# Which half of a block's queries and keys comes last: piece order and GpSimd's copies in a segment-recurrent attention kernel

## The chip, the cores and the metric

The kernel runs on one core of a Trainium2 chip. The metric is the device time of one execution in microseconds (us). The core's engines each follow an instruction stream of their own and meet through semaphores: TensorE (PE; its weight loads are shown as PEld), VectorE (DVE), ScalarE (ACT), GpSimd (POOL) and SyncE (SP). DMAs are issued from the queues of SP and GpSimd.

## The reference

The input x is 2048 x 512, in bf16. Two kinds of layer alternate, each twice: x + A(layernorm(x)), then x + B(layernorm(x)).

Layer A is attention over segments with a recurrent memory. The 2048 tokens are cut into 64 segments of 32. A memory of 8 rows stands ahead of each segment. Cut to what matters:

```python
for s in range(64):
    h = concat([mem, x[32*s:32*s+32]])          # 40 rows
    q, k, v = (einsum('btd,dhe->bhte', h, W) for W in (Wq, Wk, Wv))   # 32 heads of 128
    p = softmax(where(mask, q @ k.T * scale, -1e9))
    o = einsum('bhte,hed->btd', p @ v, Wo)
    mem, out[s] = o[:8], o[8:]
```

The memory that segment s + 1 reads is the result of segment s, so the 64 segments form a chain. Only the memory rows depend on the segment before: queries, keys and values of token rows can be computed ahead.

Layer B is a gated MLP: a projection with a GELU, a layernorm of one half, a 2048 x 2048 product over the rows, a product with the other half, and a projection back.

## The kernel before

One program does A, B, A, B. `a_block` is layer A and `b_block` layer B; the change lies in `a_block`, so it acts in both passes over it.

**Segments and blocks.** `a_block` loops over the 64 segments s. Four of them make a block of 128 tokens (`tb = s // 4`, `j4 = s % 4`); there are 16 blocks. The function `segment` computes one segment with all 32 heads. The heads are handled as two halves of 16 (r = 0 and 1). A segment works on a window of 32 rows: the 8 memory rows and the first 24 token rows. The last 8 token rows of each segment don't pass through this window: they are gathered over the four segments of a block (`hB`, 32 rows) and projected for the whole block ahead of time. The text calls that result a block's queries, keys and values: QTB, KTB and VB, both halves in each.

**Scores.** `scores(r)` makes the scores of half r on TensorE: sixteen small matmuls (L975) whose moving operand is QQ, all 40 query columns of a head, and four (L979) with the stationary operand KX[r], the last 8 keys of the segment. Each segment calls `scores(0)`, does a part of the value projection, and calls `scores(1)`. The mask product (`close`, L987, VectorE) and the sums and values follow.

**What fills QQ and KX.** Columns 0 to 31 of QQ come from the window, by a VectorE transpose in `qk_T` (L952). Columns 32 to 39 and KX come from the block's QTB and KTB, by three copies in `prep_segment`: QQ (both halves of the queries in one instruction, L905), KX[0] and KX[1] (L909). They run on GpSimd (for the very first segment of the program on VectorE). QQ and the two KX exist twice and alternate with the segments, so the copies for segment s + 2 can begin when segment s has made its scores.

**The pieces.** A block's projections are six pieces, numbered j: 0 and 1 are the halves of the queries, 2 and 3 the halves of the keys, 4 and 5 the halves of the values. A piece is sixteen matmuls (`b_mms`, L714, tile psb); ScalarE copies the result to `rowsB` (L763), and it is transposed into QTB or KTB in one of two ways: by a DMA transpose that SP issues (L768), or by VectorE (L766, called a turn; it is put on the list `turns`, and `run(turns)` near the end of the segment issues it). The pieces are written out by generators. A segment calls `fill()` three times, and each call runs its generator to the next `yield`; so pieces are spread over the four segments of the block before the one that will use them. `b_even` serves blocks 0 to 3 of a pass (which prepare 1 to 4), except the first pass's block 0: seven block boundaries in all. In each pair of segments one piece is "quartered", its four contraction steps at the first two fills of each segment, and two pieces are whole, each at the third fill. The whole piece at the last fill of a block is the one that VectorE turns. From block 4 on `b_units` does it, with another spread, and every piece is transposed by DMA.

Before the change the last two segments of `b_even` hold piece 2 (quartered), piece 1 (whole, by DMA) and piece 3 (whole, turned).

**What sets the order of instructions.** On TensorE, VectorE and ScalarE the order is the program's own, written out by hand (`ORDERED`, `tc.manual_schedule`). On GpSimd and SP the framework's scheduler sets it, within what the data dependencies allow; each engine then issues in that order and waits at the head of its queue.

Of the kernel before, what the change touches and what calls it, by code (L numbers as in the profile page):

```python
# [16 lines left out]
KT = 4  # L17
# [564 lines left out]
def qk_rhs(w, j, kt, cg):  # L582
    return w[j // 2][:, kt, :].rearrange("p (r gs i eb el) -> p r eb i gs el", r=2, gs=4, i=4, eb=4)[:, j % 2, cg]


def cols_rhs(w, j, kt, cg):
    at = 2048 * (j % 2) + 512 * cg
    return w[j // 2][:, kt, at:at + 512]
# [81 lines left out]
def a_block(tc, c, rows, front, MV_in, RS_in, MV_out, RS_out, ahead, wo, S, first):  # L670
# [6 lines left out]
    with ExitStack() as ctx:  # L677
# [34 lines left out]
        def mm_chunk(ps, lhs, rhs, kts=range(KT)):  # L712

            return [nc.tensor.matmul(ps[32 * cg:32 * cg + 32, :], lhsT=lhs(kt, cg), rhs=rhs(kt, cg), start=(kt == 0), stop=(kt == KT - 1),  # L714
                                     tile_position=(0, 32 * cg)) for kt in kts for cg in range(4)]
# [10 lines left out]
        QQr = [pers.tile([P, 2, 8, 40, 2], BF16, name=f"QQ{i}") for i in range(NKQ)]  # L726
        KXr = [[pers.tile([P, 4, 32], BF16, name=f"KX{i}{r}") for r in range(2)] for i in range(NKQ)]
        uT = [pers.tile([P, H, 32], BF16, name=f"uT{i}") for i in range(2)]
# [8 lines left out]
        def store_v(bs):  # L737
            nc.sync.dma_start(rows.vb_d[:], bs["VB"].rearrange("p i r e -> p (i r e)"))
# [8 lines left out]
        copies, turns, adds = [], [], []  # L747
# [5 lines left out]
        def b_out(bs, slot, j, ps, turned, stored):  # L753

            if j >= 4:
                nc.scalar.copy(bs["VB"][:, :, j - 4, :], ps.rearrange("p (i e) -> p i e", i=4))
                if turned:
                    ahead.regroup(bs["VB"], bs["VX"], (j - 4,))
                elif stored:
                    store_v(bs)  # L760
                return
            r = rowsB[:, slot, :]
            nc.scalar.copy(r, ps)  # L763
            t = bs[("QTB", "KTB")[j // 2]][:, j % 2]
            if turned:
                turns.append(lambda: nc.vector.transpose(out=t.rearrange("p a b -> p (a b)"), in_=r))  # L766
            else:
                nc.sync.dma_start_transpose(out=t.rearrange("p (i g) k -> p i (g k)", g=4), in_=r.rearrange("t (i e) -> t i e", i=4))  # L768

        def b_mms(bs, j, ps, kts, turned=False):  # L770
            mm_chunk(ps, lambda kt, cg: bs["hB"][:, kt, :],
                     lambda kt, cg: qk_rhs(w, j, kt, cg) if j < 4 and turned else cols_rhs(w, j, kt, cg), kts)
# [23 lines left out]
        def b_even(tb):  # L796

            bs = blk_state[tb]
            for j, others in ((4, (5, 0)), (2, (1, 3))):
                psA = accA.tile([P, 512], F32, name="psb")[:]  # L800
                for kt, other in zip((0, 2), others):
                    b_mms(bs, j, psA, (kt,))
                    yield
                    b_mms(bs, j, psA, (kt + 1,))
                    if kt == 2:
                        copies.append(lambda j=j, psA=psA: b_out(bs, 0, j, psA, False, True))
                    yield
                    psB = accB.tile([P, 512], F32, name="psb")[:]
                    b_mms(bs, other, psB, range(KT), other == 3)
                    copies.insert(0, lambda other=other, psB=psB: b_out(bs, 1, other, psB, other == 3, False))  # L810
                    yield

        def wo_pairs(px, lhs):
# [87 lines left out]
        def prep_segment(s, eng=nc.gpsimd):  # L901
            tb, j4 = s // 4, s % 4
            bs = blk_state[tb]
            QQ = QQr[s % NKQ]
            eng.tensor_copy(QQ[:].rearrange("p r n q two -> p (r n) two q")[:, :, :, 32:40],  # L905
                            bs["QTB"].rearrange("p r (n two) k -> p (r n) two k", two=2)[:, :, :, 8 * j4:8 * j4 + 8])
            KX = KXr[s % NKQ]
            for r in range(2):
                eng.tensor_copy(KX[r][:].rearrange("p g (k i) -> p i g k", i=4),  # L909
                                      bs["KTB"][:, r].rearrange("p (i g) k -> p i g k", i=4)[:, :, :, 8 * j4:8 * j4 + 8])  # L910
            seg_state[s] = dict(QQ=QQ, KX=KX, VX=bs["VX"])

# [19 lines left out]
        def segment(s, fill, spare1, spare2, spare3, tail, loads):  # L932
            tb, j4 = s // 4, s % 4
            st = seg_state.pop(s)
            QQ, KX, VX = st["QQ"], st["KX"], st["VX"]
            KA = KAr[s % 2]
# [20 lines left out]
            def ends(q):  # L957

                return q.rearrange("p h (b e) -> p h b e", e=8)[:, :, 0:5:4, :]

            def own(q):

                return q.rearrange("p (i b e) -> p i b e", i=4, b=2)
# [4 lines left out]
            def scores(r):  # L968
# [8 lines left out]
                for g in range(4):  # L977
                    q = QQ[:, r].rearrange("p (i g) q two -> p i g two q", i=4)[:, :, g // 2, g % 2, :]
                    mms.append(nc.tensor.matmul(own(pS[32 * g:32 * g + 32, 160:224]), lhsT=KX[r][:, g, :], rhs=ends(q),  # L979
                                                start=False, stop=True, tile_position=(0, 32 * g), skip_group_check=True))  # L980
# [162 lines left out]
            if s + 1 < NSEG:  # L1143
                prep_segment(s + 1)
# [14 lines left out]
        start = nc.vector if first else nc.gpsimd  # L1159
        rows.begin(start)  # L1160
        prep_segment(0, start)
        due, ys = [], []
        seen = pers.tile([P, 1], BF16, name="seen")
# [16 lines left out]
        for s in range(NSEG):  # L1180
            tb, j4 = s // 4, s % 4
# [149 lines left out]
```

## Time and profile before

| | |
|---|---|
| three runs, median (lowest to highest) | 1624.81 us (1623.7 to 1625.13) |
| the profiled execution | 1621.89 us |
| its span | 1620.2 us |
| granted TensorE clock, mean | 0.998 |
| TensorE busy | 1577.7 us, 97% |
| VectorE busy | 1070.7 us, 66% |
| ScalarE busy | 1050.1 us, 65% |
| GpSimd busy | 288.2 us, 18% |

The profile is of one execution. Times in it count from the start of its span; the execution's own time has some 1.7 us more around it. A row of the view in order of time reads: start in us, duration in us, engine, line of the kernel, operation, what it writes <- what it reads, partitions x elements, how many instructions are merged, and in brackets how long the engine sat idle before it and what ended that. A row of the waits reads: who waited <- for whom: us in total, times, longest. A row of the groups reads: busy us, mean ns of one | idle before it. "POOL" is GpSimd, "SPq" the queue of SyncE. Buffer numbers are left out of names; "old" and "front" are the memory that QTB, KTB and VB of odd and even blocks lie in, so "KX<-old" is a key copy and "old<-rowsB" a transposed piece.

Segment s of a pass begins its scores at the first of its L975 matmuls. Segments of the first blocks take 9.67 us each.

### The profile page before, as it was taken

How to read it: one execution, taken by the hardware profiler on the slowest of the kernel's cores; microseconds unless marked ns; L12 is line 12 of the kernel's file. 1: busy time of each engine (PE TensorE's matmuls, PEld its weight loads, DVE VectorE, ACT ScalarE, POOL GpSimd, SP SyncE). 2: the span in 40 equal slices, each digit the busy share in tenths (PEclk: the TensorE clock that was granted, in tenths of full speed). 3: DMA queues.
4: the chain of work that ended last, by engine and by line, in shares of the span. 5: the costliest groups of instructions: out<-in, count | busy, mean ns of one | idle time of the engine just before them, and what ended most of it. 6: DMA issues, size and time to landing. Idle time of an engine off the chain costs nothing.

```text
span 1620.2 us, 91261 instructions
## 1 busy us (share of the span) xinstructions
PE 1577.7 (97%) x41182; PEld 983.8 (61%) x41182; DVE 1070.7 (66%) x3059; ACT 1050.1 (65%) x2281; POOL 288.2 (18%) x604
## 2 busy tenths in 40 slices
PE   5899999999999999999999999999999999999999
PEld 2566666666666666566656656666666666665565
DVE  4576766667776776784366666666677667768622
ACT  3677777777777777660047777777777777776400
POOL 6111111112211221320011111111121112214000
PEclk9999999999999999999999999999999999999999
DMA  9412111113321333277952122121233223425696
GB/s 364 94 42 41 41 44 43 43 43 83 74 56 44 89 83 78 92 184 157 203 161 47 46 42 50 46 47 47 72 87 77 47 69 99 99 52 172 144 197 160
DMA packets 259805, 148.11 MB, mean 91 GB/s; under 512 B 193752, under 2 KB 235840, under 8 KB 259416
## 3 DMA queue, kind: packets, MB, share of 16 engines
q1 hardware_dynamic: 246184, 98.46, 27.8%
q0 software_dynamic: 13232, 43.82, 8.3%
q8 instruction: 322, 5.28, 1.4%
q14 instruction: 67, 0.55, 0.1%
HBM read 59.68 MB, written 37.19 MB: 60 GB/s over the span
## 4 chain that ended last, share of the span: by engine, by line
PE 50%; DMA 4%; DVE 2%; issue 0%; SPq 0%; ACT 0%; POOL 0%; DVEq 0%; ACTq 0%
PE psK L714 6%; PE psQ L714 6%; PE pg L397 5%; PE psb L714 5%; PE pz L296 5%; PE psO L825 4%; PE px L818 3%; PE psV L714 3%; PE psm L714 3%; PE pwB L837 2%; PE psO L1024 2%; PE psT L1016 1%; PE py L440 1%; DMA y_x<-xd 1%; DMA ln_x<-xd 1%; PE psS L975 1%
## 5 line engine op out<-in xcount | busy, mean ns | idle before, releaser
L714 PEld LDWEIGHTS <-hT 128*32 128x32 bf16 x12288 | 343.8, 97 | 265.3 <-DVE hT L924 14.0
L714 PE MATMUL psV<-Wv_sb,hT 128*32 128x512 bf16 x2048 | 165.7, 379 | 0.0
L952 DVE STREAM_TRANSPOSE QQ<-rows 128x256 f32<-128x256 f32 x256 | 113.1, 442 | 77.8 <-ACT rows L949 75.8
L949 ACT CAST rows<-psQ 128x512 bf16<-128x512 f32 x256 | 144.2, 592 | 27.6 <-PE psQ L714 24.9
L984 ACT ACTIVATE S<-psS 128x224 bf16<-128x224 f32 x256 | 92.2, 360 | 100.7 <-PE psS L979 100.5
L1045 DVE TENSOR_TENSOR uT<-psO,Rm 128x128 bf16<-128x128 f32 x256 | 74.7, 292 | 123.0 <-ACT Rm L1042 122.0
L397 PE MATMUL pg<-z,wspT 128*128 128x344 bf16 x1024 | 154.3, 309 | 0.0
L1048 DVE TENSOR_TENSOR uT<-psO,Rt 128x384 bf16<-128x384 f32 x256 | 140.4, 548 | 19.2 <-ACT Rt L1124 17.0
L952 DVE STREAM_TRANSPOSE KA<-rows 128x256 f32<-128x256 f32 x256 | 113.6, 444 | 59.5 <-ACT rows L949 56.4
L714 PE MATMUL psK<-Wv_sb,hT 128*32 128x512 bf16 x2048 | 152.0, 378 | 0.0
L1124 ACT ACTIVATE Rt<-Rt 128x512 f32<-128x512 f32 x256 | 147.3, 622 | 4.0
L825 PE MATMUL psO<-Wo_high,uT 128*32 128x128 bf16 x8192 | 140.2, 219 | 3.8 <-issue 3.7
L714 PE MATMUL psQ<-Wq_sb,hT 128*32 128x512 bf16 x2048 | 136.0, 381 | 7.1 <-DVE xo L448 2.5
L714 PE MATMUL psQ<-Wk_sb,hT 128*32 128x512 bf16 x2048 | 135.3, 380 | 0.0
L714 PE MATMUL psK<-Wk_sb,hT 128*32 128x512 bf16 x2048 | 134.8, 379 | 0.0
L714 PE MATMUL psm<-Wq_sb,hT 128*32 128x512 bf16 x2048 | 134.8, 379 | 0.0
L818 PE MATMUL px<-Wo,uT 128*32 128x256 bf16 x3840 | 133.2, 273 | 0.4
L1121 ACT ACTIVATE Rt<-psT 128x1024 f32<-128x1024 f32 x128 | 131.2, 1025 | 3.2
L397 PEld LDWEIGHTS <-wspT 128*128 128x128 bf16 x1024 | 100.2, 98 | 53.2
L825 PEld LDWEIGHTS <-uT 128*32 128x32 bf16 x8192 | 125.9, 97 | 10.4 <-issue 5.4
L818 PEld LDWEIGHTS <-uT 128*32 128x32 bf16 x4096 | 107.0, 97 | 27.0 <-DVE uT L1045 1.3
L909 POOL COPY KX<-old 128x128 bf16<-128x128 bf16 x128 | 66.0, 535 | 312.1 <-PE psS L979 194.9
(200 smaller groups left out, 2864.7 us busy)
## 6 DMA issues: line engine op xcount, KB each, us to landing
o_d<-o_sb SPq DMA_DIRECT2D x126, 64.0 KB
vb_d<-front SPq DMA_DIRECT2D x30, 256.0 KB
VX<-vb_d SPq DMA_DIRECT2D x120, 64.0 KB
ln_x<-xd SPq DMA_DIRECT2D x26, 256.0 KB
y_o<-o_d POOLq DMA_DIRECT2D x22, 256.0 KB, 3.5
xd<-y_o POOLq DMA_DIRECT2D x22, 256.0 KB, 2.9
Wq_sb<-in_A_Wq_dram POOLq DMA_DIRECT2D x8, 512.0 KB, 8.2
Wk_sb<-in_A_Wk_dram POOLq DMA_DIRECT2D x8, 512.0 KB, 10.0
```

The costliest lines, as they stand in the source:

```text
L296: nc.tensor.matmul(pz[:, c0:c1], lhsT=xnT[:, kt, :], rhs=w_in_sb[:, kt, c0:c1], start=(kt == 0), stop=(kt == KT - 1))
L397: nc.tensor.matmul(pg[t][:, k, 0:344], lhsT=wsp[t][:, st, :], rhs=z(st, 344 * k, 344 * k + 344), start=(st == 0), stop=(st == NT - 1))
L714: return [nc.tensor.matmul(ps[32 * cg:32 * cg + 32, :], lhsT=lhs(kt, cg), rhs=rhs(kt, cg), start=(kt == 0), stop=(kt == KT - 1), tile_posi ...
L818: nc.tensor.matmul(px[at:at + 32, 0:256], lhsT=lhs[:, h, :], rhs=wo_rhs(h, slice(k + 2, None, -2) if h % 2 else slice(k, None, 2)), start= ...
L825: nc.tensor.matmul(pw[32 * cg:32 * cg + 32, :], lhsT=lhs[:, h, :], rhs=wo_rhs(h, cg), start=False, stop=(h == H - 1), tile_position=(0, 32 ...
L949: return r, mms, copy(r[:].rearrange("p (n el two) -> p n el two", n=8, two=2), ps.rearrange("p (n two el) -> p n el two", n=8, two=2))
L952: nc.vector.transpose(out=(QQ[:, j % 2, :, 0:32] if j < 2 else KA[:, j % 2]).bitcast(F32).rearrange("p n q one -> p n (q one)"), in_=r[:]. ...
L984: return nc.scalar.activation(out=S[:, r], in_=psS[:, r, 0:224], func=ACT.Exp, scale=scale)
L1045: nc.vector.tensor_tensor(out=hview(uT_cur[:], r, 24, 32), in0=oview(r, 0, 8), in1=Rm[:, r].rearrange("p g (n q) -> p g n q", q=8), op=ALU ...
L1048: nc.vector.tensor_tensor(out=hview(uT_nxt[:], r, 0, 24), in0=oview(r, 8, 32), in1=rview(r, 0, 24), op=ALU.mult)
L1121: nc.scalar.activation(out=Rt[:], in_=psT[:], func=ACT.Ln)
L1124: nc.scalar.activation(out=rt, in_=rt, func=ACT.Exp, scale=-1.0)
```

## The change

Two edits in `a_block`.

In `b_even` the pieces of the last two segments change places. Piece 3 (half 1's keys) is now the quartered one, whose DMA transpose is the last to be issued in the block. Piece 2 (half 0's keys) is whole, at the third fill of the third segment, and by DMA. Piece 1 (half 1's queries) is whole at the last fill, and VectorE turns it.

In `prep_segment`, for segments with j4 of 0 or 1, one more copy of a single column (128 x 1) reads the new columns of QQ and writes one column of KX[1], which the copy of the keys overwrites afterwards. It makes a data dependency: the copy into KX[1] comes behind the copy into QQ in GpSimd's order. The results of the kernel don't depend on the value.

```diff
         def b_even(tb):
 
             bs = blk_state[tb]
-            for j, others in ((4, (5, 0)), (2, (1, 3))):
+            for j, others in ((4, (5, 0)), (3, (2, 1))):
                 psA = accA.tile([P, 512], F32, name="psb")[:]
                 for kt, other in zip((0, 2), others):
...
                     psB = accB.tile([P, 512], F32, name="psb")[:]
-                    b_mms(bs, other, psB, range(KT), other == 3)
-                    copies.insert(0, lambda other=other, psB=psB: b_out(bs, 1, other, psB, other == 3, False))
+                    b_mms(bs, other, psB, range(KT), other == 1)
+                    copies.insert(0, lambda other=other, psB=psB: b_out(bs, 1, other, psB, other == 1, False))
                     yield
...
             KX = KXr[s % NKQ]
+            if j4 < 2:
+                eng.tensor_copy(KX[1][:, 0, 0:1], QQ[:, 0, 0, 32:33, 0])
             for r in range(2):
                 eng.tensor_copy(KX[r][:].rearrange("p g (k i) -> p i g k", i=4),
```

In the changed program TensorE, VectorE, ScalarE and SP issue the same kinds of instructions in the same order as before, apart from one added column copy on VectorE at the start. On GpSimd there are 63 more. At the seven boundaries GpSimd's order before was: two QQ copies, the copy of hB, KX[0] of the next two segments, KX[1] of the next two. Now it is: KX[0] of the next two segments, hB, the two QQ copies, and then for each of the two segments the column copy and KX[1]. In later blocks KX[0], KX[1], QQ becomes KX[0], QQ, the column copy, KX[1].

## The prediction

> **What bounds the kernel now.** I read the page first, then the waits of TensorE, then the order of time around the seven places that the change touches.
>
> ```profile
> span 1620.2 us, 91261 instructions
> PE 1577.7 (97%) x41182; PEld 983.8 (61%) x41182; DVE 1070.7 (66%) x3059; ACT 1050.1 (65%) x2281; POOL 288.2 (18%) x604
> PE 50%; DMA 4%; DVE 2%; issue 0%; SPq 0%; ACT 0%; POOL 0%; DVEq 0%; ACTq 0%
> PE psS L979 <- POOL KX L909: 4.7, 5, 1.6
> PE psO L825 <- issue: 3.7, 8, 1.3
> ```
>
> TensorE is busy 97% of the span, so only what removes or adds TensorE idle time counts. The last two lines are from the waits of TensorE: the largest one that lies between segments is that of the memory-key scores (L979) for GpSimd's key copy (L909): 4.7 us in five waits. "Issue" is no wait for another engine. Next, in order of time: an ordinary segment, then the first segment of a block whose projections the changed generator made.
>
> ```profile
> 113.81 0.28 PE L975 MATMUL psS<-QQ,KA 128*32 128x40 bf16 x16
> 113.91 0.21 PE L979 MATMUL psS<-QQ,KX 128*32 128x64 bf16 x4
> 115.02 0.28 PE L975 MATMUL psS<-QQ,KA 128*32 128x40 bf16 x16
> 115.12 0.21 PE L979 MATMUL psS<-QQ,KX 128*32 128x64 bf16 x4
> ...
> 119.86 1.21 SPq L768 DMA_TRANSPOSE front<-rowsB  x1
> 120.35 0.29 POOL L637 COPY hB<-hT 128x128 bf16<-128x128 bf16 x1 [4.36 <-DMA hT<-ln_xn]
> 121.56 0.70 DVE L766 STREAM_TRANSPOSE front<-rowsB 128x512 bf16<-128x512 bf16 x1
> 123.48 0.28 PE L975 MATMUL psS<-QQ,KA 128*32 128x40 bf16 x16
> 124.11 1.64 POOL L909 COPY KX<-front 128x128 bf16<-128x128 bf16 x5 [3.46 <-DMA front<-rowsB]
> 124.63 0.21 PE L979 MATMUL psS<-QQ,KX 128*32 128x64 bf16 x4 [0.86 <-POOL KX L909]
> ```
>
> In the ordinary segment L979 of half 0 starts 0.10 us behind the first score matmul, and that of half 1 starts 115.12 - 113.81 = 1.31 us behind it. At the block's first segment half 0's keys (piece 2, issued by SP at 119.86) land at about 124.1; GpSimd copies them; L979 starts 0.52 us after that copy began, 1.15 behind the first score matmul instead of 0.10. VectorE's turn of the other piece (L766) was over at 122.26. So piece 2, by DMA, ends this wait. The other six boundaries:
>
> ```profile
> 163.32 0.28 PE L975 MATMUL psS<-QQ,KA 128*32 128x40 bf16 x16
> 163.43 0.21 PE L979 MATMUL psS<-QQ,KX 128*32 128x64 bf16 x4
> ...
> 202.03 0.28 PE L975 MATMUL psS<-QQ,KA 128*32 128x40 bf16 x16
> 203.12 1.63 POOL L909 COPY KX<-front 128x128 bf16<-128x128 bf16 x5 [3.61 <-DMA front<-rowsB]
> 203.65 0.21 PE L979 MATMUL psS<-QQ,KX 128*32 128x64 bf16 x4 [1.34 <-POOL KX L909]
> ...
> 875.07 0.28 PE L975 MATMUL psS<-QQ,KA 128*32 128x40 bf16 x16
> 875.95 0.21 PE L979 MATMUL psS<-QQ,KX 128*32 128x64 bf16 x4 [0.60 <-POOL KX L909]
> ...
> 914.53 0.28 PE L975 MATMUL psS<-QQ,KA 128*32 128x40 bf16 x16
> 915.13 0.21 PE L979 MATMUL psS<-QQ,KX 128*32 128x64 bf16 x4 [0.32 <-POOL KX L909]
> ...
> 951.85 0.70 DVE L766 STREAM_TRANSPOSE old<-rowsB 128x512 bf16<-128x512 bf16 x1
> 953.77 0.28 PE L975 MATMUL psS<-QQ,KA 128*32 128x40 bf16 x16
> 955.14 1.63 POOL L909 COPY KX<-old 128x128 bf16<-128x128 bf16 x5 [3.60 <-DMA old<-rowsB]
> 955.66 0.21 PE L979 MATMUL psS<-QQ,KX 128*32 128x64 bf16 x4 [1.60 <-POOL KX L909]
> ...
> 995.20 0.28 PE L975 MATMUL psS<-QQ,KA 128*32 128x40 bf16 x16
> 995.42 0.21 PE L979 MATMUL psS<-QQ,KX 128*32 128x64 bf16 x4
> ```
>
> The delay of each is the distance of its two starts less 0.10: 1.05 (the first), 0.01, 1.52, 0.78, 0.50, 1.79 and 0.12: 5.77 us together. I use this sum and not the 4.7 of the waits, because the end of the matmuls before is modelled and the starts are recorded.
>
> **The change part by part.** *The late piece becomes half 1's keys (piece 3 by DMA in place of piece 2).* As many matmuls, ScalarE copies and DMA transposes are issued at the same places of the same queues, SP's included; so I let the late keys land when they did. They are still GpSimd's first copy after the landing, so L979 could start when it did. But half 1's L979 needs them only 1.31 us behind the first score matmul, 1.21 later than half 0's. Each delay w becomes max(0, w - 1.21): zero at five boundaries, 1.52 - 1.21 = 0.31 at 202 and 1.79 - 1.21 = 0.58 at 953. What is left is 0.89; gained are 5.77 - 0.89 = 4.88 us. Half 0's keys (piece 2) are now projected whole a segment earlier, with their DMA behind them, and nothing is late for it.
>
> *VectorE turns half 1's queries.* The turn keeps its 0.70 us and its place. New is what hangs on it: GpSimd's query copy (L905) reads both halves of the queries, and all sixteen L975 read the copied columns. Formerly it ran a segment earlier. Now it stands behind the turn, and behind the copy of hB (L637), which ended at 120.64 and is no later than the turn. Its parts:
>
> ```profile
> 827.80 1.44 DVE L664 STREAM_TRANSPOSE front<-ln_xn 128x512 bf16<-128x512 bf16 x2
> 829.30 0.76 POOL L909 COPY KX<-front 128x128 bf16<-128x128 bf16 x2 [3.19 <-DVE front L664]
> 115.52 0.48 POOL L905 COPY QQ<-front 128x256 bf16<-128x256 bf16 x1 [0.89 <-PE psS L979]
> ```
>
> GpSimd starts 0.06 us after a VectorE transpose (829.24 to 829.30), the query copy takes 0.48, and TensorE follows some 0.05 after it (a key copy begins at 124.11, L979 0.52 later, of which 0.47 is the copy: an estimate from the groups' 1.64 for five overlapping ones). That is 0.59 us from the turn's end to the first score matmul. At hand are 123.48 - 122.26 = 1.22, and as much at 953.77 - 952.55. It costs nothing; 0.63 us of cover is left. If the cover goes, L975 of half 0 is what is late, one for one, at seven boundaries.
>
> *The one-column copies.* One per segment with j4 below 2: 64, one of them on VectorE at the very start. Each reads the fresh QQ and writes KX[1], so half 1's key copy waits for the query copy. The nearest row is the same form on the same engine:
>
> ```profile
> L1203 POOL COPY seen<-E 128x1 bf16<-128x1 bf16 x6 | 1.2, 202 | 0.0
> 234.44 0.48 POOL L909 COPY KX<-old 128x128 bf16<-128x128 bf16 x1 [9.78 <-DMA old<-rowsB]
> 235.84 0.61 POOL L905 COPY QQ<-old 128x256 bf16<-128x256 bf16 x1 [0.92 <-DMA old<-rowsB]
> 243.77 0.27 PE L975 MATMUL psS<-QQ,KA 128*32 128x40 bf16 x16
> ```
>
> 63 x 0.202 = 12.7 us on an engine that is busy 18%. At a changed boundary two of them stand between the query copies and the late keys: 122.80 + 0.39 (the second query copy) + 0.20 is about 123.4, ahead of the landing at 124.1. In later blocks, as in the last three rows, half 1's keys were copied at 234.44, ahead of the queries at 235.84; now they come behind them, near 237, for use at about 245. Both are hidden. The cover would have to lose some 8 us.
>
> *GpSimd beside VectorE.* More copies now fall near the mask product of half 1 (L987), on which the next TensorE work hangs:
>
> ```profile
> 115.81 0.39 DVE L987 TENSOR_TENSOR E<-S,maskN 128x448 bf16<-128x448 bf16 x1
> 987.26 0.47 POOL L905 COPY QQ<-front 128x256 bf16<-128x256 bf16 x1 [0.29 <-PE psS L998]
> 987.27 0.65 DVE L987 TENSOR_TENSOR E<-S,maskN 128x448 bf16<-128x448 bf16 x1
> ```
>
> A copy that began 0.01 us ahead of L987 made it 0.65 instead of 0.39; one that began 0.29 ahead (115.52, above) did nothing. The price of a hit is 0.26 us, bounds 0 and 0.26 at each of seven boundaries: 0 to 1.8. I take 0, as in the ordinary segment, and keep 1.8 for the range. Below nothing it can't be, except for such hits that go: the 987.27 one stems from early query copies, which move.
>
> The Trainium skill ("SBUF — State Buffer", section "Who interferes with whom") states that a VectorE instruction with two SBUF inputs and a GpSimd instruction that reads SBUF block each other for the whole instruction, whichever issues first. By that alone the product at 987.27 would have taken about 0.46 + 0.39 = 0.85 and the one at 115.81 would have waited too; the trace has 0.65 and 0.39, so the rows decide.
>
> The sum: -4.88 us. Against the profiled execution's own 1621.89 us this makes 1617.0. The three runs' median is 1624.81, 2.9 us above that execution; taken from it, the forecast is 1619.9 us, 0.30% faster. About 0.2% (3.25 us) is what a measurement can tell from no change.
>
> **The rivals.** *The gain is smaller than can be told.* The gain is the sum of min(w, 1.21), and w is how late a DMA lands: 0.01 to 1.79 in seven boundaries of one execution. Were every w half as large, the gain would be 0.53 + 0.01 + 0.76 + 0.39 + 0.25 + 0.90 + 0.06 = 2.90 and the time 1621.9. For it: five of seven delays are under 1.1. Against: both layers show large ones. Chance 0.17; this holds the case that keys and queries just change places as the last to come.
>
> *The turned queries become the wait.* Place: L975 at seven boundaries. With x us from the turn's end to the first score matmul, each loses x - 1.22; the loss passes 4.88 + 3.25 us, and the kernel is told slower, from x = 1.22 + 8.13 / 7 = 2.4 us on. At x = 3 it is 7 x 1.78 - 4.88 = 7.6 us slower: 1632.4. Against it stand the rows that make x 0.59. Chance 0.04.
>
> *GpSimd blocks VectorE's product.* Each of the 63 new copies that begins just ahead of L987 costs up to 0.26 us; from (4.88 + 3.25) / 0.26 = 31 hits on it is slower. If all hit, 63 x 0.26 = 16.4, so 11.5 us slower: 1636.3. Against: most of these copies run where the row at 235.84 does, behind the product. Chance 0.04. This rival is where the rule of the Trainium skill above would lead if it held strictly.
>
> **How the numbers follow.** The forecast has 0.75. Its own range is 1617.5 to 1621.5: with every w doubled the gain is 1.21 x 4 + 1.00 + 0.24 + 0.02 = 6.1 (1618.7), and I go 1.2 us lower for landings later than any in this execution. The range of 8 in 10 takes in the halved delays and the 1.8 us of hits: 1621.9 + 1.8 = 1623.7, so 1617.0 to 1624.0. Faster 0.75, same 0.17, slower 0.08.
>
> **What would show it.** After the change, the waits of TensorE for KX should hold under 1.5 us, all at half 1's L979, and the first L979 of a block should start 0.10 behind L975. L905 at the seven boundaries should start within 0.1 us of L766's end and end 0.5 us or more ahead of L975. Wrong would be: a wait of L975 for L905; half 1's L979 waiting over 0.6 us at most boundaries (late keys landing later than now); L987 at 0.5 to 0.65 us in many segments.

## The result, and the profile after

The changed kernel takes 1619.26 us (median; 1615.93 to 1624.08) where the kernel before, run beside it, takes 1623.99 (1619.25 to 1626.44). The ratio is 0.9974, with a 95% interval of 0.9965 to 0.9982: 4.7 us between the medians, where the prediction had 4.88. The profiled execution took 1618.1 us, 3.8 less than that of before.

In the changed kernel the added lines shift the numbers: the score matmuls are L977 (was L975) and L981 (was L979), the key copies L911 (was L909), the mask product L989 (was L987), the sums that follow it L1018 (was L1016). L909 is now the one-column copy. The page and a row of the waits of TensorE:

```profile
span 1616.4 us, 91216 instructions
PE 1578.8 (98%) x41182; PEld 983.8 (61%) x41182; DVE 1069.0 (66%) x3060; ACT 1048.9 (65%) x2281; POOL 301.6 (19%) x667
...
PE psS L981 <- POOL KX L909: 0.7, 2, 0.5
```

TensorE has the same 41182 matmuls and fills 98% of a shorter span. The wait of the memory-key scores for GpSimd's key copies, 4.7 us in five waits before, is 0.7 us in two. The first changed boundary, in order of time, with rows of other work left out:

```profile
120.48 1.21 SPq L768 DMA_TRANSPOSE front<-rowsB  x1
...
122.05 0.70 DVE L766 STREAM_TRANSPOSE front<-rowsB 128x512 bf16<-128x512 bf16 x1
122.81 0.85 POOL L905 COPY QQ<-front 128x256 bf16<-128x256 bf16 x2 [1.55 <-DVE front L766]
123.58 0.19 POOL L909 COPY KX<-QQ 128x1 bf16<-128x1 bf16 x1
123.97 0.28 PE L977 MATMUL psS<-QQ,KA 128*32 128x40 bf16 x16
124.08 0.21 PE L981 MATMUL psS<-QQ,KX 128*32 128x64 bf16 x4
124.98 0.35 DVE L989 TENSOR_TENSOR E<-S,maskN 128x448 bf16<-128x448 bf16 x1
125.00 0.65 POOL L911 COPY KX<-front 128x128 bf16<-128x128 bf16 x1 [1.24 <-DMA front<-rowsB]
125.18 0.28 PE L977 MATMUL psS<-QQ,KA 128*32 128x40 bf16 x16
125.71 0.21 PE L981 MATMUL psS<-QQ,KX 128*32 128x64 bf16 x4 [0.25 <-POOL KX L909]
```

The turn ends at 122.75; GpSimd copies the queries from 122.81 on, then the one column, and stands ready before the late keys land at about 125.0. L981 of half 0 starts 0.11 behind L977. L981 of half 1, at 125.71, is the one that waits: 0.53 behind its own L977 at 125.18 instead of 0.10, so 0.43 late. (The row names L909 as what ended the wait; the copy that ran until 125.65 is L911. It took 0.65 instead of 0.48: it began 0.02 behind half 0's mask product, L989 at 124.98, and 0.17 of the 0.43 comes from that.) Two other boundaries, the third and the sixth:

```profile
201.98 0.28 PE L977 MATMUL psS<-QQ,KA 128*32 128x40 bf16 x16
202.08 0.22 PE L981 MATMUL psS<-QQ,KX 128*32 128x64 bf16 x4
...
203.30 0.21 PE L981 MATMUL psS<-QQ,KX 128*32 128x64 bf16 x4
...
953.67 0.28 PE L977 MATMUL psS<-QQ,KA 128*32 128x40 bf16 x16
953.89 0.47 POOL L911 COPY KX<-old 128x128 bf16<-128x128 bf16 x1 [1.64 <-DMA old<-rowsB]
954.41 0.21 PE L981 MATMUL psS<-QQ,KX 128*32 128x64 bf16 x4 [0.46 <-POOL KX L909]
```

At the third nothing is late (half 1's L981 starts 1.32 us behind the first score matmul, as in an ordinary segment); at the sixth half 1's L981 starts 0.74 behind its L977, 0.64 late. Over the seven boundaries half 1 is late by 0.43, 0, 0, 0.11, 0, 0.64 and 0: 1.2 us. Half 0's L981 is nowhere late. Before, the seven delays were 5.77 us together, so 4.6 us of delay are gone at the boundaries.

### The profile page after: what moved, and what is told of

Read it like the earlier page. It is cut to its first block, busy times and chain, and to the rows that moved or that the text cites. A ratio compares the mean times of both kernels' runs of the same rounds, so it can differ in the third digit from the quotient of the medians.

```text
span 1616.4 us, 91216 instructions
## 1 busy us (share of the span) xinstructions
PE 1578.8 (98%) x41182; PEld 983.8 (61%) x41182; DVE 1069.0 (66%) x3060; ACT 1048.9 (65%) x2281; POOL 301.6 (19%) x667
## 4 chain that ended last, share of the span: by engine, by line
PE 55%; DVE 1%; issue 1%; DMA 0%; ACT 0%; POOL 0%; POOLq 0%; DVEq 0%
PE pg L397 9%; PE psQ L714 7%; PE psK L714 7%; PE psb L714 5%; PE pz L296 5%; PE psO L825 3%; PE px L818 3%; PE psV L714 3%; PE psm L714 3%; PE py L440 2%; PE pwB L837 2%; PE psO L1026 2%; PE psT L1018 1%; PE psS L977 1%; PE pw L1285 0%
## 5 line engine op out<-in xcount | busy, mean ns | idle before, releaser
L1047 DVE TENSOR_TENSOR uT<-psO,Rm 128x128 bf16<-128x128 f32 x256 | 74.6, 291 | 123.4 <-ACT Rm L1044 123.0
L825 PE MATMUL psO<-Wo_high,uT 128*32 128x128 bf16 x8192 | 140.0, 219 | 2.3 <-issue 2.0
L825 PEld LDWEIGHTS <-uT 128*32 128x32 bf16 x8192 | 125.7, 97 | 8.6 <-issue 4.2
L911 POOL COPY KX<-old 128x128 bf16<-128x128 bf16 x128 | 65.3, 539 | 275.4 <-PE psS L981 211.0
```

The lines of the kernel that those rows point to most:

```text
L825: nc.tensor.matmul(pw[32 * cg:32 * cg + 32, :], lhsT=lhs[:, h, :], rhs=wo_rhs(h, cg), start=False, stop=(h == H - 1), tile_position=(0, 32 ...
L1047: nc.vector.tensor_tensor(out=hview(uT_cur[:], r, 24, 32), in0=oview(r, 0, 8), in1=Rm[:, r].rearrange("p g (n q) -> p g n q", q=8), op=ALU ...
```

## The experiments

Two theories are to be told apart. **Slack:** the late transfer lands as before, and the gain is that half 1 needs it 1.21 us later than half 0. **Turn:** the gain comes from which piece VectorE turns, or from the other order of GpSimd's copies. The runs were made on two chips, four kernels on each, with the kernel before beside them; its medians there were 1629.89 and 1624.88 us, so only ratios are compared.

**1. The new piece order without the one-column copies** (order_alone). Against the changed kernel:

```diff
-            if j4 < 2:
-                eng.tensor_copy(KX[1][:, 0, 0:1], QQ[:, 0, 0, 32:33, 0])
```

> The pieces change places as in the change, the one-column copies are left out. GpSimd's order at the seven boundaries is then KX[0] of two segments, hB, KX[1] of two segments, and behind them the two QQ copies, so the queries wait for the landing of the late keys. My theory (the gain needs the late keys behind everything that half 0's scores read): the first score matmul (L975) waits until landing + 0.78 (two key copies) + 0.53 (query copy and hand-over). With the landings of the profile before (0.63, -0.46, 1.09, 0.36, 0.09, 1.37 and -0.32 us from the first score matmul) these waits are 1.94, 0.85, 2.40, 1.67, 1.40, 2.68 and 0.99, together 11.9 us instead of 5.8: 6 us slower than before, ratio 1.004. Rival (the order of the pieces is the whole gain, the copies do nothing): 4.7 us faster, ratio 0.997.

Measured: ratio 1.0027 (1.0011 to 1.0044), slower than before. Order of time at the first boundary, and the wait:

```profile
121.71 0.70 DVE L766 STREAM_TRANSPOSE front<-rowsB 128x512 bf16<-128x512 bf16 x1
...
124.91 0.75 POOL L909 COPY KX<-front 128x128 bf16<-128x128 bf16 x2 [3.94 <-DMA front<-rowsB]
125.46 0.87 POOL L905 COPY QQ<-front 128x256 bf16<-128x256 bf16 x2
125.99 0.28 PE L975 MATMUL psS<-QQ,KA 128*32 128x40 bf16 x16 [2.17 <-POOL QQ L905]
...
PE psS L975 <- POOL QQ L905: 11.1, 6, 2.5
```

The queries were ready at 122.41, but GpSimd stood 3.94 us before the late keys, with the query copies behind them in its queue. From the distances of starts L975 is 12.3 us late over the seven boundaries. So the piece order alone loses; the column copy is no small cost that rides along but what makes the rest work.

**2. The one-column copies without the new piece order** (copies_alone). Against the kernel before:

```diff
             KX = KXr[s % NKQ]
+            if j4 < 2:
+                eng.tensor_copy(KX[1][:, 0, 0:1], QQ[:, 0, 0, 32:33, 0])
```

> The kernel before with the 64 one-column copies added and nothing else. My theory: each 0.2 us lies on an idle stretch of GpSimd, half 0's keys still come last and end the same waits (5.8 us): ratio 1.000, within 0.001. Rival (the order of GpSimd's copies is itself the gain): 0.997. Rival (the copies cost TensorE time by blocking VectorE's mask product, 0.26 us a hit, 63 copies): up to 1.010.

Measured: ratio 1.000 (0.9986 to 1.0013).

```profile
L909 POOL COPY KX<-QQ 128x1 bf16<-128x1 bf16 x63 | 14.2, 226 | 3.7
...
PE psS L981 <- POOL KX L911: 5.5, 5, 1.8
```

The 14.2 us that GpSimd spends on the columns are hidden, and half 0's late keys still cost 6.7 us by starts. The copies, and the order that they make, bring nothing by themselves.

**3. Half 1's keys late, but VectorE turns half 0's keys instead of half 1's queries** (keys_turned_ordered). An ordering column keeps half 1's late keys behind half 0's turned ones. Against the changed kernel:

```diff
-            for j, others in ((4, (5, 0)), (3, (2, 1))):
+            for j, others in ((4, (5, 0)), (3, (1, 2))):
...
-                    b_mms(bs, other, psB, range(KT), other == 1)
-                    copies.insert(0, lambda other=other, psB=psB: b_out(bs, 1, other, psB, other == 1, False))
+                    b_mms(bs, other, psB, range(KT), other == 2)
+                    copies.insert(0, lambda other=other, psB=psB: b_out(bs, 1, other, psB, other == 2, False))
...
-            if j4 < 2:
-                eng.tensor_copy(KX[1][:, 0, 0:1], QQ[:, 0, 0, 32:33, 0])
             for r in range(2):
+                if r == 1 and j4 < 2:
+                    eng.tensor_copy(KX[1][:, 0, 0:1], KX[0][:, 0, 0:1])
```

> Piece 3 (half 1's keys) is the late one as in the change, but VectorE turns piece 2 (half 0's keys) and both query halves come early by DMA; the one-column copy orders KX[1] behind KX[0] instead of behind QQ. My theory (what counts is that the late piece is one that scores(1) alone reads; what VectorE turns is indifferent as long as GpSimd's copy of it is in time, here 0.59 us for 1.32): the same gain as the change, 4 to 5 us, ratio 0.997. Rival (that the queries moved to VectorE is part of the gain): no gain, 1.000.

Measured: ratio 0.9975 (0.9956 to 0.9993), the gain of the change. The first boundary:

```profile
126.30 0.28 PE L977 MATMUL psS<-QQ,KA 128*32 128x40 bf16 x16
126.41 0.21 PE L981 MATMUL psS<-QQ,KX 128*32 128x64 bf16 x4
126.68 0.48 POOL L911 COPY KX<-front 128x128 bf16<-128x128 bf16 x1 [0.77 <-DMA front<-rowsB]
...
127.61 0.21 PE L981 MATMUL psS<-QQ,KX 128*32 128x64 bf16 x4
...
PE psS L981 <- POOL KX L910: 1.8, 1, 1.8
```

The late keys are copied at 126.68, 0.38 behind the first score matmul; half 0 would have waited for them, half 1 doesn't. 2.2 us of waits are left. Which of the two pieces VectorE turns makes no difference that these times show.

**4. Half 1's queries late, VectorE turns half 1's keys** (queries_late), without one-column copies:

```diff
-            for j, others in ((4, (5, 0)), (3, (2, 1))):
+            for j, others in ((4, (5, 0)), (1, (2, 3))):
```

with the turn at `other == 3` again.

> The quartered piece that ends last holds half 1's queries (piece 1), piece 2 (half 0's keys) is whole and early, VectorE turns half 1's keys as before. No one-column copies; GpSimd's order puts QQ ahead of KX[1] by itself. My theory: all of half 0's score matmuls read the copied columns of QQ, so the late piece now holds up the first of them, 0.10 us earlier than half 0's keys did: waits of 1.16, 0.07, 1.62, 0.89, 0.62, 1.90 and 0.21, together 6.5 us; 0.7 us slower than before, ratio 1.000 (0.999 to 1.001). Rival (any piece but half 0's keys may come last, since queries of half 1 are needed by scores(1) only): as the change, 0.997.

Measured: ratio 1.0004 (0.9989 to 1.002).

```profile
126.69 0.87 POOL L905 COPY QQ<-front 128x256 bf16<-128x256 bf16 x2 [3.50 <-DMA front<-rowsB]
127.21 0.28 PE L975 MATMUL psS<-QQ,KA 128*32 128x40 bf16 x16 [1.09 <-POOL QQ L905]
...
PE psS L975 <- POOL QQ L905: 6.9, 6, 2.3
```

One copy fills both halves' queries, so half 1's late queries hold up half 0's first score matmul: 8.1 us by starts. This is the rival in which keys and queries merely change places. It isn't the piece that matters but when what hangs on it is first needed.

**5 and 6. The landing made later, in both kernels** (before_late, after_late). Two plain DMAs that nothing reads are issued ahead of the late piece's transpose, in the queue of SyncE:

```diff
+                if stored:
+                    for d in rows.spare_d:
+                        nc.sync.dma_start(d[:], r)
```

> The kernel before; SP issues two more DMAs (the late piece's rows to two spare DRAM buffers) right ahead of the late piece's transpose, so half 0's keys land later by some 1.2 us (two issues of about 0.6 each, as the plain loads on SP show). My theory: every boundary loses the whole delay, since L979 of half 0 has no slack: the waits grow from 5.8 to about 14 us, 8 us slower than before, ratio 1.005. If the landing isn't what ends the wait: 1.000.

> The changed kernel with the same two DMAs ahead of its late piece (half 1's keys). My theory: the wait at each boundary is max(0, delay - 1.21), with a delay 1.2 us larger than now; so the two late kernels differ by up to 7 x 1.21 = 8.5 us where the two without the DMAs differ by 4.7: this one takes about 6 us of waits at half 1's L979, 5 us more than the change has now, and ends at about the time of the kernel before, ratio 1.000. Rival (the change removes the wait altogether, whatever the landing): no loss against the change, 0.997.

Measured: before_late 1.0044 (1.0027 to 1.0062), after_late 0.9994 (0.9981 to 1.0008). Added lines make the score matmuls L979 and L983 in the first, L981 and L985 in the second. Order of time at the third boundary, and the waits, first of before_late:

```profile
199.53 0.84 SPq L771 DMA_DIRECT2D spare_d<-rowsB  x2
...
202.76 0.28 PE L979 MATMUL psS<-QQ,KA 128*32 128x40 bf16 x16
204.13 1.64 POOL L913 COPY KX<-front 128x128 bf16<-128x128 bf16 x5 [3.81 <-DMA front<-rowsB]
204.65 0.21 PE L983 MATMUL psS<-QQ,KX 128*32 128x64 bf16 x4 [1.60 <-POOL KX L913]
...
PE psS L983 <- POOL KX L913: 8.5, 7, 2.3
```

then of after_late:

```profile
205.71 0.29 PE L981 MATMUL psS<-QQ,KA 128*32 128x40 bf16 x16
205.81 0.21 PE L985 MATMUL psS<-QQ,KX 128*32 128x64 bf16 x4
206.93 0.28 PE L981 MATMUL psS<-QQ,KA 128*32 128x40 bf16 x16
207.79 0.47 POOL L915 COPY KX<-front 128x128 bf16<-128x128 bf16 x1 [2.27 <-DMA front<-rowsB]
208.31 0.21 PE L985 MATMUL psS<-QQ,KX 128*32 128x64 bf16 x4 [1.11 <-POOL KX L913]
...
PE psS L985 <- POOL KX L913: 4.6, 5, 1.9
```

In before_late half 0 is late by 1.36, 0.51, 1.79, 1.16, 0.69, 2.52 and 1.78, 9.8 us together; the expected 14 took a delay of 1.2 us per boundary, and on average (9.8 - 5.77) / 7 = 0.6 came, so the size was wrong. In after_late half 0 is nowhere late. There the late copies begin 1.52, 0.41, 2.08, 1.62, 0.41, 2.89 and 1.33 us behind the first score matmul. With 0.52 us from the copy's start to L985, the delays should be that plus 0.52 less 1.31: 0.73, 0, 1.29, 0.83, 0, 2.10 and 0.54. Measured are 0.73, 0, 1.29, 0.83, 0, 2.10 and 0.55. So the slack of 1.21 us holds at each of the five boundaries where the keys are late enough to tell. Between the two late kernels lie 0.0050, some 8.1 us, of which their waits explain 9.8 - 5.5 = 4.3. The length of the two segments round each boundary, from the first score matmul of the one ahead to that of the second one behind, is over the seven boundaries 148.33 us in before_late and 142.95 in after_late. This gap of 5.4 is more than the waits tell, for one thing because at the sixth boundary of before_late half 1's scores, too, start 0.37 later than half 0's wait explains. The rest, some 2.7 us, stays open.

**7. The query copies made later** (queries_delayed). Against the changed kernel, in the first two segments of blocks 1 to 4, ahead of the query copy:

```diff
+            if j4 < 2 and 0 < tb < 5:
+                for _ in range(2 - 2 * j4):
+                    eng.tensor_copy(whole[:], bs["QTB"][:, 1].rearrange("p h k -> p (h k)"))
+                eng.tensor_copy(QQ[:, 0, 0, 32:33, 0], whole[:, 0:1])
```

> The changed kernel with work put between VectorE's turn and GpSimd's query copy at the boundaries: two copies of 128 x 512 to a spare tile, which the query copies then have to wait for (by a copy of one column each). From the 0.48 us of a 128 x 256 copy I estimate 0.6 to 0.9 for each, with the column copies about 2 us in all. My theory (0.63 us of cover between the query copy and the first score matmul): L975 gets late by about 1.3 us at seven boundaries; the late keys are then in time by themselves. 8 us slower than the change, ratio to before about 1.002. Rival (the queries have much more room, since some other wait stands ahead of L975): as the change, 0.997.

Measured: ratio 1.0005 (0.9994 to 1.0015), 0.0037 or 6.0 us above the change on the same chip. The score matmuls are L982 here.

```profile
122.81 1.29 POOL L908 COPY whole<-front 128x512 bf16<-128x512 bf16 x2 [2.07 <-DVE front L766]
...
124.42 0.86 POOL L910 COPY QQ<-front 128x256 bf16<-128x256 bf16 x2
124.95 0.28 PE L982 MATMUL psS<-QQ,KA 128*32 128x40 bf16 x16 [0.79 <-POOL QQ L910]
...
PE psS L982 <- POOL QQ L910: 5.3, 7, 0.8
```

The query copies start at 124.42, 1.61 later than the 122.81 of the change. TensorE is 0.98, 0.86, 0.98, 0.98, 0.98, 0.97 and 0.90 late: 6.6 us. (The expected 1.3 each took 2 us of added work for the 1.61 that came.) From the copy's start to the matmul the queries need 124.95 - 124.42 = 0.53. The change has 123.97 - 122.81 = 1.16 for it, so it leaves 0.63 us of cover, and a delay of 1.61 should cost 0.98. It does at most boundaries: beyond the cover a delay costs its full length. With half 1's keys late by 0.94 here and 1.65 in the next run, the waits make 6.6 - 0.7 = 5.9 us, and the time says 6.0, give or take two or three.

**8. The change again, on this chip** (after_again).

> The change unaltered, on the same chip as the three others, as their reference: 0.997 of the kernel before, with 1 to 2 us of waits left at half 1's L979.

Measured: ratio 0.9968 (0.9955 to 0.9981). Waits and order of time at the sixth boundary:

```profile
953.05 0.28 PE L977 MATMUL psS<-QQ,KA 128*32 128x40 bf16 x16
...
955.49 0.47 POOL L911 COPY KX<-old 128x128 bf16<-128x128 bf16 x1 [2.64 <-DMA old<-rowsB]
...
PE psS L981 <- POOL KX L909: 1.5, 1, 1.5
```

Only this boundary still waits, by 1.65 us: its keys were copied 2.44 behind the first score matmul. It was the latest one in the kernel before, too.

The wait that is left, 1.2 to 1.7 us, is 0.1% of the time, less than these measurements tell from nothing; none of the kernels here is told faster than the change.

## Why the prediction was right

**The late piece becomes half 1's keys.** The step held. The slack of 1.21 us, read from one ordinary segment, is what after_late shows at five boundaries. The residue was 1.2 us in the profile of the change and 1.65 in after_again, for 0.89 predicted. That the late keys "land when they did" is true only on average: the key copy began 1.37 us behind the first score matmul at the sixth boundary before, 1.43 and 2.44 in the two profiles of the change, with the issue at the same place of the queue. In after_again that one boundary makes the whole residue, in the first profile 0.64 of the 1.2, so its size is luck.

**VectorE turns half 1's queries.** Right, to 0.01 us: GpSimd starts 0.06 behind the turn at all seven boundaries, and 0.63 us of cover is left, as predicted. The rival of the turned queries, with its price of one for one beyond the cover, is what queries_delayed built.

**The one-column copies.** They cost nothing, as predicted, at 0.218 us each instead of 0.202. But the prediction priced only their presence. It noted that they put half 1's keys behind the queries, without working out what happens if they aren't there: 12.3 us of waits, and a slower kernel. That was missing among its steps; it didn't touch the sum, because the change has them. It also has a small sum wrong: one column copy, not two, stands between the query copies and the first late keys, and it ended at 123.77, not at about 123.4, since the two query copies take 0.85 us from 122.81 on and not 0.39. It stayed hidden, 1.2 us ahead of the keys.

**GpSimd beside VectorE.** Taken as nothing, with 0 to 1.8 us as bounds. Hits on the product of half 1 did come at three changed boundaries. Order of time of the changed kernel, from three places:

```profile
126.30 0.49 POOL L905 COPY QQ<-front 128x256 bf16<-128x256 bf16 x1
126.37 0.61 DVE L989 TENSOR_TENSOR E<-S,maskN 128x448 bf16<-128x448 bf16 x1 [0.44 <-ACT S L986]
127.04 0.45 PE L1018 MATMUL psT<-E,ones 64*128 64x512 bf16 x4
...
875.86 0.39 DVE L989 TENSOR_TENSOR E<-S,maskN 128x448 bf16<-128x448 bf16 x1
875.88 0.70 POOL L905 COPY QQ<-old 128x256 bf16<-128x256 bf16 x1
...
994.39 0.47 DVE L989 TENSOR_TENSOR E<-S,maskN 128x448 bf16<-128x448 bf16 x1
```

The product of half 1 took 0.61 instead of 0.39 behind a query copy that began 0.07 ahead of it, 0.62 at the sixth boundary, and 0.47 at the last; TensorE's L1018 starts 0.06 behind its end. That is 0.22 + 0.23 + 0.08 = 0.5 us, inside the bounds. Elsewhere such hits went, the one at 987.27 among them: over all 128 segments, half 1's products longer than 0.40 us are together 0.6 us over the usual 0.39 both before and after. So nothing was right in sum, and by compensation. The prediction had such meetings cost the product alone; at the first boundary the late key copy paid, with the 0.17 us above.

**What isn't accounted for.** At the boundaries 4.6 us of delay went, in the span 3.8. The pairs of segments round the seven boundaries, from start to start as above, are together 142.8 us long before and 139.0 in the profile of the change, as in after_again: 3.8 less. So some 0.7 us was lost again inside these pairs. In the profile of the change most of it lies in the first segment behind the fourth boundary, where TensorE stands ahead of L825 for nothing that the profile shows:

```profile
879.37 0.55 PE L825 MATMUL psO<-Wo_high,uT 128*32 128x128 bf16 x25 [0.56 <-issue]
```

From there on that segment runs 0.8 us later than in after_again, which has no such wait there; waits of this kind lie elsewhere in each execution (3.7 us in eight before, 2.0 in five after). Outside the pairs the differences go both ways, up to 1.2 us, and come to nothing in sum. One of them lies ahead of all boundaries: the segment ahead of the first changed boundary starts at 114.31 instead of 113.81:

```profile
114.31 0.28 PE L977 MATMUL psS<-QQ,KA 128*32 128x40 bf16 x16
```

This 0.5 us comes from the start of the program, which the change doesn't touch but for one column copy. In after_again, the same kernel, that segment starts at 116.78, so it is scatter. Between two executions of one kernel on one chip lie several us (1617.55 to 1620.66 in after_again), so a single pair of profiles doesn't settle a us. That the medians came within 0.2 us of the forecast is luck, too: the interval of the ratio reaches from 2.9 to 5.7 us of gain, and the boundaries themselves show 3.8.

**The rivals.** Smaller gain: the medians are 4.7 us apart in the one comparison and 5.7 in the other; only the upper ends of the intervals, 0.9982 and 0.9981, come near its 2.9 us. Turned queries as the wait: refuted by their 0.63 us of cover. Blocking by GpSimd: five of half 1's 128 products took over 0.40 us where six did before, not 31 more.

## What to carry to other kernels

When a transfer lands late by a scattering amount, find which consumer needs it first and give the late place to the data that is needed last; the gain is at most the sum of min(delay, slack) over the places (here 4.6 us of delay went, and the segments round the boundaries got 3.8 shorter), and the slack can be read from an undisturbed stage. On an engine whose order a scheduler sets, moving data also moves what queues behind the late landing: work that is ready can stand behind it, and a tiny copy that makes a dependency puts it ahead (here the difference between 1.0027 and 0.9974). Ask of such an ordering instruction not only what it costs but what the order is without it.

## What the runs showed of the hardware

The time from SyncE's issue of a transposing DMA to GpSimd's copy isn't a constant: 4.5 us at the first boundary above (120.48 to 125.00), and over the seven boundaries 3.65 to 4.37 before, and up to 5.26 in after_again. Two more DMAs ahead of it in its queue took 0.84 us to issue, but made the keys only some 0.6 us later on average, by TensorE's delays.

Which of two meeting instructions on GpSimd and VectorE is stretched goes by who began first, to within some hundredths of a us: the copy ahead by 0.07 us stretched the product (0.61 for 0.39), the product ahead by 0.02 us stretched the copy (0.70 for 0.48) and was itself unharmed; but a key copy that began 0.01 us ahead of half 0's product, at 993.39 of the change, was itself stretched (0.71). How much the product loses goes by the head start. It ended 0.66 us behind the start of the query copy when that was 0.01 ahead (987.26, before), 0.68 behind it at 0.07 (126.30) and at 0.21 (the copy before 994.39 began at 994.18), and also 0.68 behind it at 0.29, where it lost nothing (115.52, before). All ten profiles have it so: 0.66 to 0.71 in the 45 places where a query copy began 0.01 to 0.25 ahead and the product lost time. Less the product's own 0.39, a query copy of 0.48 us holds it up during its first 0.3 us or so and no longer; why wasn't tested. The Trainium skill ("SBUF — State Buffer", section "Who interferes with whom") states that issue order decides who blocks, and that the other blocks fully; the trace agrees with the first but for starts that close together. A full block until the copy's end at 126.79 would have made the product 0.42 + 0.39 = 0.81 us, and it took 0.61.

The mean granted clock of TensorE went with the waits: on the first chip 0.9965 on average in order_alone and 0.9978 in keys_turned_ordered, on the second 0.9960 in before_late and 0.9977 in after_again. A thousandth of the 1580 us that TensorE is busy is about 1.6 us (an estimate), so some of the gaps between kernels may lie there. Whether the waits lower the clock or something else does wasn't tested.
